# Clustered attention and a gated convolution FFN on one core: q loaded with three tokens in a row to a partition, and exponentials that write their columns back into sequence

## The chip, the core and the metric

The kernel runs on one core of a Trainium2 chip. The metric is the device time in microseconds (us) of one execution. The core has TensorE (PE, with its weight loads shown apart as PEld), VectorE (DVE), ScalarE (ACT), GpSimd (POOL), SyncE (SP), which here only issues DMAs, and 16 DMA engines.

## The reference

Four batches, eight heads, 768 tokens, head size 64. Each token of q and of k belongs to the nearest of 16 centroids of its head; a query sees the keys of its own cluster only. The output of the attention goes through a feed-forward layer with a convolution over three tokens and a gate.

```python
q_assign = np.argmax(np.einsum('bhsd,hcd->bhsc', q_n, c_n), axis=-1)
k_assign = np.argmax(np.einsum('bhsd,hcd->bhsc', k_n, c_n), axis=-1)
mask = q_assign[:, :, :, None] == k_assign[:, :, None, :]
scores = np.where(mask, scale * np.matmul(q, k.transpose(0, 1, 3, 2)), -1e9)
attn = softmax(scores)                       # over the keys
x = np.matmul(attn, v)                       # heads put side by side: 512 columns
h = np.maximum(x @ w_in, 0.0)                # 1024 columns
conv_out = conv_w[0] * h[s-1] + conv_w[1] * h[s] + conv_w[2] * h[s+1]
out = (h * sigmoid(conv_out)) @ w_out
```

The order of the keys does not matter as long as k and v have the same one. The order of the queries is that of the output, and of the convolution.

## The kernel before

**Pairs and slots.** The work goes by pairs of heads: pair g is two heads of one batch, 16 pairs in all. A slot t is half of the queries (384, HS) of one pair, 32 slots in all; `slot` gives a slot's batch, half a, and pair. Batch 0 is slots 0 to 7 and batch 1 slots 8 to 15. Each slot has six steps i: head i // 3, and a third of the keys (two blocks of 128).

**Loads and transposes.** q and k come from the device's memory with tokens on partitions (qk_in) and are needed with the 64 columns of a head on partitions (qkT, then ext in f16). Two ways lead there. Pairs 7 to 15 (`in_blocks`, those for which the plan has an LZ step) are loaded as blocks of 32 by 32 and turned by VectorE (L298). Pairs 0 to 6 are loaded by `load_q` and `load_k` (L255 and L263), transposed by TensorE (`transposes`, L309), 128 tokens of two blocks at a time, copied from PSUM to qkT by ScalarE or VectorE (L315, L317), and cast into ext (L330). For these seven pairs k is loaded with six tokens in a row to a partition, so that k's columns in ext are in a permuted order, and v alike (L279). q is loaded token by token: partition p gets the tokens p, 128 + p, 256 + p and so on, and the columns of q are in sequence.

**Clusters.** The argmax over the centroids (L347 to L389) runs on the columns as they stand, and three more rows of ext (partitions 64 to 66) carry the cluster of each token, so that a matmul of ext with ext gives the masked score; the partitions behind are zero.

**Scores, exponentials, values.** `scores` (L437) multiplies two blocks of keys by the 384 queries of the slot into one of two PSUM tiles sc, in turn. `exps` (L450) takes exp of such a tile, 128 x 768 values, into two rows of attn in f16 (L454). `values` (L461) loads 128 columns of attn as weights and multiplies them by v, so that the 128 queries of a column block become the partitions of the result (L466); `normalize` divides by the sum, and a transpose brings x to xT, whose columns are tokens in sequence. The feed-forward layer (L520 on) reads xT.

**What sets the order.** PLAN is one list of steps written out; each engine runs the instructions of its steps in that order, and each queue of DMAs is in that order too. Nothing reorders them. In PLAN, LQ and L are loads of q (and k), T transposes, Qa and Qd the copies to qkT, CD the casts into ext, S scores, E exponentials, V values, LV and CV the load and cast of v. The first step of the plan is the load of q of pair 0, head 0.

Of the kernel before, what the change touches and what calls it, by code (L numbers as in the profile page):

```python
# [10 lines left out]
AF = mybir.ActivationFunctionType  # L11
# [144 lines left out]
def kernel(  # L156
# [11 lines left out]
    nc = tc.nc  # L168
    B, H, S, D = q.shape
    P = 128  # L170
# [6 lines left out]
    HS = S // 2  # L177
# [2 lines left out]
    SPB = 2 * NPR  # L180
    NU = 2 * NPR
    BR = 3
    SHARP = 24.0


# [11 lines left out]
    sc = [psum.tile([P, 2, 512], F32, name=f"sc{i}") for i in range(2)]  # L197
# [22 lines left out]
    NE = 6  # L220
    ext_b = [const.tile([P, 2, 2, S], F16, name=f"ext{i}") for i in range(NE)]
# [14 lines left out]
    def batch_pair(g):  # L236
        return g // NPR, 2 * (g % NPR)

    def heads(h):
        return slice(0, 2) if h is None else slice(h, h + 1)  # L240

    def qk_in(g):
        if g not in qk_t:
            qk_t[g] = rot.tile([P, 2, 2, J, D], F32, name="qk_in", tag="qk_in", bufs=4)
        return qk_t[g]
# [4 lines left out]
    in_blocks = [f"LZ.{g}.0" in PLAN for g in range(B * NPR)]  # L250
# [4 lines left out]
    def load_q(g, h=None, queue=nc.sync):  # L255
        b, h0 = batch_pair(g)
        hs = heads(h)
        queue.dma_start(
            qk_in(g)[:, 0, hs].rearrange("p h j d -> p (h j) d"),
            q[b, h0 + hs.start : h0 + hs.stop].rearrange("h (j p) d -> p (h j) d", p=P),  # L260
        )

    def load_k(g, h=None, queue=nc.sync):  # L263
# [55 lines left out]
    def copy(name, to, src):  # L319
        if name == "a":  # L320
            nc.scalar.activation(to, src, AF.Copy)
        else:
            (nc.vector if name == "d" else nc.gpsimd).tensor_copy(out=to, in_=src)  # L323
# [32 lines left out]
    def argmax(g, h, i):  # L356
# [24 lines left out]
        else:  # L381
# [3 lines left out]
            if i == 5:  # L385
                nc.vector.tensor_scalar(out=mid, in0=best, scalar1=-8.5, scalar2=SHARP, op0=ALU.add, op1=ALU.mult)
            else:
# [20 lines left out]
    def bias_rows(g, h, queue=nc.sync):  # L408
        n = 6 * J * (1 if h is not None else 2)
        queue.dma_start(  # L410
            ext_b[g % NE][D : D + BR, heads(h)].rearrange("r h a s -> r (h a s)"), spk_t.pop((g, h))[0:n, :]
        )


    def turn_rows(g, h, a, at):
        turn_at[g, h, a] = at
        for j in range(J):
            nc.tensor.transpose(
                bank16[at][D : D + BR, P * j : P * (j + 1)], pack_v[h][:, a : 2 * BR : 2, j], id16[:]
            )  # L420

    def rows_copy(name, g, h, a):
        copy(name, ext_b[g % NE][D : D + BR, h, a, :], bank16[turn_at[g, h, a]][D : D + BR, 0:S])

    attn, x16, x_at, av_at = {}, {}, {}, {}
# [4 lines left out]
    def slot(t):  # L432
        b, i = divmod(t, SPB)
        a, pr = SLOTS0[i] if b == 0 else divmod(i, NPR)
        return b, a, pr, b * NPR + pr

    def scores(t, i):  # L437
        b, a, pr, g = slot(t)
        h, kt = i // 3, 2 * (i % 3)
        s = sc[(6 * t + i) % 2]  # L440
        for n in range(2):
            nc.tensor.matmul(  # L442
                s[:, n, 0:HS],
                lhsT=ext_b[g % NE][:, h, 1, P * (kt + n) : P * (kt + n + 1)],
                rhs=ext_b[g % NE][:, h, 0, HS * a : HS * (a + 1)],
                start=True,
                stop=True,
            )

    def exps(t, i):  # L450
        if i % 3 == 0:
            attn[t, i // 3] = rot.tile([P, J, HS], F16, name="attn", tag="attn", bufs=4)
        kt = 2 * (i % 3)
        nc.scalar.activation(  # L454
            attn[t, i // 3][:, kt : kt + 2, :], sc[(6 * t + i) % 2][:, :, 0:HS], AF.Exp, scale=0.125
        )

    def avp(at):
        return bank[at][:, 0 : J * VW].rearrange("p (u w) -> p u w", u=J)
# [193 lines left out]
    def setup(name, i, j):  # L653
# [54 lines left out]
        elif name == "pk":  # L708
            n = pack_n[i]
            nc.gpsimd.memset(pack_b[i][:, 6 * n * J : P], 0.0)  # L710
            for h in range(n):
                nc.gpsimd.memset(pack_v[i][:, 2 * h + 1 : 2 * h + 4 * n + 1 : 4 * n - 1], -SHARP / 2)
        elif name == "v":
# [38 lines left out]
    def step(token):  # L752
# [5 lines left out]
        if name[0] == "_":  # L758
            setup(name[1:], at if at is not None else x[0] if x else 0, last)
        elif name == "L":  # L760
            load_q(x[0])
            load_k(x[0])
        elif name == "LQ":
            load_q(x[0], last)
        elif name == "LK":
            load_k(x[0], last)
# [30 lines left out]
        elif name == "BA":  # L797
            bias_rows(x[0], last, nc.scalar)
        elif name == "S":
            scores(*x)  # L800
        elif name == "E":
            exps(*x)
        elif name == "V":
            values(*x, at)
# [67 lines left out]
```

## Time and profile before

| what | value |
|---|---|
| median of 3 runs | 240.79 us (240.72 to 243.44) |
| profiled execution | 240.68 us |
| its span, first to last instruction | 238.9 us |
| granted TensorE clock over the span | 0.998 |
| exponentials (L454) | 192 of 128 x 768, 817 ns each by the mean |
| loads of q of pairs 0 to 6 | 4 of 192 KB and 5 of 384 KB |
| packets of all DMAs | 102,958, of which 94,603 under 512 B |

In the profile's rows L and a number is a line of the kernel. "out<-in" are the names of tiles without their buffer numbers. In a list of groups, "x192 | 146.4, 817 | 4.0 <-PE sc L442 2.7" reads: 192 instructions, 146.4 us busy, 817 ns each, 4.0 us in which the engine sat idle just before one of them, 2.7 of it ended by PE's writing of sc in line 442. The chain that ended last is followed back from the last instruction, at each step to what released it. "issue" is idle time for which the profile shows no releaser.

### The profile page before, as it was taken

What the parts mean: (1) busy time and instruction counts of PE and PEld (TensorE: products, weight loads), DVE (VectorE), ACT (ScalarE), POOL (GpSimd) and SP (SyncE); (2) the same over time, 40 slices, a digit from 0 to 9 for tenths busy, and PEclk for the clock granted to TensorE, in tenths of its full rate; (3) what the DMA queues carried; (4) which work ended last, traced back from release to release, by engine and by line L of the source; (5) the groups of instructions that cost most, each with busy time, mean ns of one, the idle gap of its engine ahead of it and who ended that gap; (6) DMA issues with size and microseconds to landing.
All of it is one profiled execution on the core that took longest, in us unless ns stands there. A gap on an engine that the chain in (4) does not pass through costs nothing.

```text
span 238.9 us, 6438 instructions
## 1 busy us (share of the span) xinstructions
PE 227.7 (95%) x2442; PEld 143.5 (60%) x2442; DVE 215.4 (90%) x497; ACT 215.4 (90%) x337; POOL 84.6 (35%) x149
## 2 busy tenths in 40 slices
PE   7988998999999999999999999999999999999984
PEld 4665665575556566655666666655776666555531
DVE  6999999989999999999899999999899999983850
ACT  5998997999999999999999999999999999994542
POOL 8559664790168335411935031304540001000000
PEclk9999999999999999999999999999999999999999
DMA  7988599944956975878669507890542110323104
GB/s 198 294 243 257 157 233 245 323 80 83 242 92 136 183 128 94 173 126 183 163 150 169 114 3 188 153 134 1 168 89 63 33 47 16 105 64 112 68 0 177
DMA packets 102958, 32.77 MB, mean 137 GB/s; under 512 B 94603, under 2 KB 98187, under 8 KB 102926
## 3 DMA queue, kind: packets, MB, share of 16 engines
q1 hardware_dynamic: 102599, 32.11, 57.3%
q8 instruction: 19, 0.31, 0.6%
q10 hardware_dynamic: 327, 0.24, 0.4%
q14 instruction: 13, 0.11, 0.1%
HBM read 23.11 MB, written 6.29 MB: 123 GB/s over the span
## 4 chain that ended last, share of the span: by engine, by line
PE 64%; DVE 15%; ACT 12%; POOL 5%; issue 2%; DVEq 0%; POOLq 0%
PE sc L442 17%; PE flex L524 15%; PE flex L604 14%; PE flex L466 10%; ACT attn L454 8%; PE flex L347 3%; POOL ext L323 3%; PE sc L566 3%; ACT th L584 2%; DVE best L380 1%; DVE ext L323 1%; DVE cnv L560 1%; DVE x L480 1%; PE sc L604 1%; DVE val L377 1%
## 5 line engine op out<-in xcount | busy, mean ns | idle before, releaser
L454 ACT ACTIVATE attn<-sc 128x768 f16<-128x768 f32 x192 | 146.4, 817 | 4.0 <-PE sc L442 2.7
L442 PE MATMUL sc<-ext 128*128 128x384 f16 x384 | 89.3, 325 | 3.8 <-ACT attn L454 2.1
L466 PEld LDWEIGHTS <-attn 128*128 128x128 f16 x1152 | 50.5, 97 | 15.2 <-ACT attn L454 0.4
L560 DVE SCALAR_TENSOR_TENSOR cnv<-hpad,cwcol,cnv 128x382 f16<-128x382 f16 (+1 forms) x100 | 58.4, 609 | 0.4
L323 POOL CAST ext<-qkT 64x768 f16<-64x768 f32 x48 | 41.7, 875 | 40.6 <-DVE qkT L298 20.0
L466 PE MATMUL flex<-v,attn 128*128 128x65 f16 x1152 | 54.5, 193 | 0.3 <-ACT attn L454 0.3
L524 PE MATMUL flex<-xT,w_in 128*128 128x384 f16 x256 | 49.1, 326 | 0.1
L442 PEld LDWEIGHTS <-ext 128*128 128x128 f16 x384 | 32.5, 97 | 26.9 <-issue 9.2
L604 PE MATMUL flex<-w_out,hg 128*128 128x512 f16 x176 | 47.1, 379 | 0.0
L592 DVE SCALAR_TENSOR_TENSOR hg<-th,hpad 128x764 f16<-128x764 f32 (+2 forms) x33 | 30.7, 934 | 3.1 <-ACT th L584 3.0
L524 PEld LDWEIGHTS <-w_in 128*128 128x128 f16 x256 | 23.9, 98 | 15.6 <-issue 0.6
L604 PEld LDWEIGHTS <-hg 128*128 128x128 f16 x192 | 17.9, 98 | 16.8 <-DVE hg L592 1.1
L537 ACT ACTIVATE hpad<-flex 128x384 f16<-128x384 f32 x45 | 21.8, 501 | 2.4 <-PE flex L524 1.6
L323 POOL CAST v<-v_in 128x768 f16<-128x768 f32 x15 | 14.6, 977 | 24.7 <-DMA v_in<-in_v_dram 24.6
L584 ACT ACTIVATE th<-cnv 128x764 f32<-128x764 f16 (+1 forms) x25 | 21.2, 848 | 0.7 <-DVE cnv L560 0.7
L323 POOL COPY hpad<-hf 128x6 f16<-128x6 f16 x12 | 4.9, 418 | 42.0 <-DVE hg L592 41.8
L480 DVE TENSOR_TENSOR x<-flex,rec 128x384 f16<-128x384 f32 x32 | 17.8, 558 | 1.1
L298 DVE STREAM_TRANSPOSE qkT<-qk_in 128x768 f32<-128x768 f32 x18 | 17.3, 966 | 0.0
L558 DVE TENSOR_SCALAR cnv<-hpad,cwcol 128x382 f16<-128x382 f16 (+1 forms) x50 | 16.3, 349 | 0.6 <-ACT hpad L537 0.5
L323 POOL COPY hf<-hpad 128x6 f16<-128x6 f16 x11 | 3.6, 329 | 30.7 <-ACT hpad L537 18.6
L347 PE MATMUL flex<-qkT,cT 128*32 128x192 f32 x256 | 14.1, 333 | 0.0
L309 PE MATMUL flex<-id,qk_in 128*128 128x128 f32 x84 | 12.5, 287 | 1.2 <-ACT qkT L315 0.6
(82 smaller groups left out, 217.1 us busy)
## 6 DMA issues: line engine op xcount, KB each, us to landing
v_in<-in_v_dram SPq DMA_DIRECT2D x16, 384.0 KB
out_dram<-o_sb SPq DMA_DIRECT2D x24, 256.0 KB
qk_in<-in_q_dram SPq DMA_DIRECT2D x36, 96.0 KB
qk_in<-in_k_dram SPq DMA_DIRECT2D x36, 96.0 KB
qk_in<-in_q_dram SPq DMA_DIRECT2D x5, 384.0 KB
qk_in<-in_k_dram SPq DMA_DIRECT2D x5, 384.0 KB
w_sb<-in_moe_w_out_dram SPq DMA_DIRECT2D x2, 768.0 KB
w_sb<-in_moe_w_in_dram SPq DMA_DIRECT2D x3, 512.0 KB
```

The lines of the kernel that those rows point to most:

```text
L323: (nc.vector if name == "d" else nc.gpsimd).tensor_copy(out=to, in_=src)
L347: nc.tensor.matmul(bank[at][32 * j : 32 * (j + 1), 192 * i : 192 * (i + 1)], lhsT=cT32[:, which, :], rhs=tokens[:, j], start=True, stop=Tr ...
L442: nc.tensor.matmul(s[:, n, 0:HS], lhsT=ext_b[g % NE][:, h, 1, P * (kt + n) : P * (kt + n + 1)], rhs=ext_b[g % NE][:, h, 0, HS * a : HS * ( ...
L454: nc.scalar.activation(attn[t, i // 3][:, kt : kt + 2, :], sc[(6 * t + i) % 2][:, :, 0:HS], AF.Exp, scale=0.125)
L466: nc.tensor.matmul(avp(at)[:, u, 0 : D + 1], lhsT=attn[t, h][:, kt, P * jq : P * (jq + 1)], rhs=v16_b[g % NE][:, h, kt, 0 : D + 1], start= ...
L480: nc.vector.tensor_tensor(out=x16[t].rearrange("p jq (h d) -> p h jq d", h=2), in0=av[:, :, 0:D].rearrange("p (h jq) d -> p h jq d", h=2), ...
L524: nc.tensor.matmul(bank[at][:, 0:HS], lhsT=w_in16[:, r, 2 * u + f, :], rhs=xT[:, b % 2, r, HS * a : HS * (a + 1)], start=(r == 0), stop=(r ...
L537: nc.scalar.activation(to, src, AF.Relu)
L560: nc.vector.scalar_tensor_tensor(out=cnv, in0=src, scalar=w, in1=cnv, op0=ALU.mult, op1=ALU.add)
L584: nc.scalar.activation(th_t[n][:, fs, 0:N], pre[:, fs, 0:N], AF.Tanh, scale=0.5)
L592: nc.vector.scalar_tensor_tensor(out=hg_b[b][:, 2 * u + fs.start : 2 * u + fs.stop, LO[a] : LO[a] + N], in0=th_t[n][:, fs, 0:N], scalar=1. ...
L604: nc.tensor.matmul(bank[at][:, 0:Dm], lhsT=hg_b[b][:, fb, P * tq : P * (tq + 1)], rhs=w_out16[:, fb, :], start=(fb == 0), stop=(fb == NFB ...
```

## The change

Three edits, of which the second leaves the operand as it was (KR is 128).

```diff
+    KR = P
...
         queue.dma_start(
-            qk_in(g)[:, 0, hs].rearrange("p h j d -> p (h j) d"),
-            q[b, h0 + hs.start : h0 + hs.stop].rearrange("h (j p) d -> p (h j) d", p=P),
+            qk_in(g)[:, 0, hs].rearrange("p h (a j) d -> p (h a) (j d)", a=2),
+            q[b, h0 + hs.start : h0 + hs.stop].rearrange("h (a p j) d -> p (h a) (j d)", a=2, j=3),
         )
...
-                lhsT=ext_b[g % NE][:, h, 1, P * (kt + n) : P * (kt + n + 1)],
-                rhs=ext_b[g % NE][:, h, 0, HS * a : HS * (a + 1)],
+                lhsT=ext_b[g % NE][0:KR, h, 1, P * (kt + n) : P * (kt + n + 1)],
+                rhs=ext_b[g % NE][0:KR, h, 0, HS * a : HS * (a + 1)],
...
-        nc.scalar.activation(
-            attn[t, i // 3][:, kt : kt + 2, :], sc[(6 * t + i) % 2][:, :, 0:HS], AF.Exp, scale=0.125
-        )
+        to, src = attn[t, i // 3][:, kt : kt + 2, :], sc[(6 * t + i) % 2][:, :, 0:HS]
+        if not in_blocks[slot(t)[3]]:
+
+            to, src = to.rearrange("p n (x j) -> p n j x", j=3), src.rearrange("p n (j x) -> p n j x", j=3)
+        nc.scalar.activation(to, src, AF.Exp, scale=0.125)
```

In each half a of the queries, partition p now holds the tokens 384 a + 3 p, + 1 and + 2, which lie behind one another in the device's memory: a packet of the load is 3 x 64 x 4 = 768 B in place of 256 B. After the transposes, column 128 j + x of the half is token 3 x + j. The scores come out in that order, and the exponential puts column (j, x) into column 3 x + j of attn. It reads PSUM in sequence and writes f16 values 6 B apart, in six runs of 128 (two blocks of keys by three j). Behind it everything is in sequence, as before. The exponentials of pairs 7 to 15 stay as they were.

No instruction is added, removed or moved on any engine. ScalarE's first exponentials, with what stands between them, before (tile names with their buffer numbers; the number at the end is the shape written):

```order
L454 ACTIVATE attn<-sc_66 128x768
L315 ACTIVATE qkT<-flex_68 128x512
L315 ACTIVATE qkT<-flex_69 128x512
L315 ACTIVATE qkT<-flex_71 128x512
L454 ACTIVATE attn<-sc_67 128x768
L454 ACTIVATE attn<-sc_66 128x768
```

and in the changed kernel:

```order
L459 ACTIVATE attn<-sc_66 128x2x3x128
L316 ACTIVATE qkT<-flex_68 128x512
L316 ACTIVATE qkT<-flex_69 128x512
L316 ACTIVATE qkT<-flex_71 128x512
L459 ACTIVATE attn<-sc_67 128x2x3x128
L459 ACTIVATE attn<-sc_66 128x2x3x128
```

Only the shape of the write is another one; the order is the same.

## The prediction

> **What bounds the kernel now.** I read the page first: the span, the engines' busy shares and the chain that ended last.
>
> ```profile
> span 238.9 us, 6438 instructions
> PE 227.7 (95%) x2442; PEld 143.5 (60%) x2442; DVE 215.4 (90%) x497; ACT 215.4 (90%) x337; POOL 84.6 (35%) x149
> ...
> PE 64%; DVE 15%; ACT 12%; POOL 5%; issue 2%; DVEq 0%; POOLq 0%
> ...
> L454 ACT ACTIVATE attn<-sc 128x768 f16<-128x768 f32 x192 | 146.4, 817 | 4.0 <-PE sc L442 2.7
> ```
>
> Three engines are busy for 90% or more of the span, so none has much slack. The exponentials (L454) are 146.4 of ScalarE's 215.4 us; all but 4.0 us of the time before them was filled. The next view is the busy time by stretches. The columns are the stretch, its length, then busy us and instruction count of PE, PEld, DVE, ACT and POOL, the granted clock, the DMA share and GB/s.
>
> ```profile
> core 0: us, PE busy (x) PEld busy (x) DVE busy (x) ACT busy (x) POOL busy (x), PEclk, DMA share, GB/s
> 0.00:12.00 12.00, 10.18 (x86) 6.50 (x86) 9.69 (x29) 9.10 (x18) 8.06 (x35) 1.00 0.94 246
> 12.00:25.00 13.00, 11.22 (x125) 7.87 (x118) 12.51 (x38) 11.82 (x20) 9.71 (x17) 1.00 0.78 233
> 25.00:40.00 15.00, 14.15 (x190) 10.22 (x187) 14.55 (x38) 14.65 (x22) 9.58 (x14) 1.00 0.91 226
> 40.00:55.00 15.00, 14.00 (x198) 9.20 (x196) 13.49 (x29) 13.80 (x21) 10.59 (x18) 1.00 0.70 184
> 55.00:70.00 15.00, 14.12 (x149) 8.48 (x147) 14.53 (x38) 14.23 (x24) 2.62 (x4) 1.00 0.73 156
> 70.00:85.00 15.00, 14.67 (x158) 9.05 (x157) 14.79 (x33) 15.00 (x24) 9.42 (x12) 1.00 0.80 153
> 85.00:100.00 15.00, 14.91 (x218) 10.36 (x215) 14.69 (x37) 14.33 (x23) 6.01 (x9) 1.00 0.68 123
> ```
>
> From 12 to 100 us, where the changed exponentials lie, ScalarE is busy 11.82 + 14.65 + 13.80 + 14.23 + 15.00 + 14.33 = 83.8 of 88 us. It has 4.2 us of idle time there. Whatever an exponential costs more than now is swallowed only up to those 4.2 us.
>
> The DMA engines are also busy, 0.94 of the first 12 us, so I asked whether anybody waits for them. The two lists below are what PE's transposes of q and k (L309) sat idle for, and the one wait of a compute engine for a load in the list of waits.
>
> ```profile
> its engine sat idle before it (us, times) until:
>   ACT qkT L315: 1.6, 2
>   DVE xT L499: 0.9, 2
>   ACT ext L321: 0.6, 2
>   issue: 0.5, 2
>   DVE sim L364: 0.3, 1
>   DVE cwcol L734: 0.3, 1
> ```
>
> ```profile
> POOL v L323 <- DMA v_in<-in_v_dram: 24.6, 6, 10.3
> ```
>
> The transposes are the only readers of q as it is loaded, and no row of theirs ends on a DMA; at most the 0.5 us of "issue", which names no releaser, could hide one. The only load that is waited for is v's, on GpSimd, which is busy 35% of the span. The chain of waits at the start says what sets it instead:
>
> ```profile
> 2.88 0.70 DVE ext L716
> 3.61 0.24 DVE sq_c L672
> 3.87 0.23 DVE nrm_c L673
> 4.13 0.20 ACT nrm_c L675
> 4.35 1.28 ACT L700
> 5.64 0.20 ACT scratch L700
> 5.84 0.39 ACT qkT L315
> ```
>
> VectorE's clearing of ext, the norm of the centroids and ScalarE's second table load come first, and the copies of q's and k's transposes (L315) start only behind that load, at 5.8 us. By then the first transposes, which ran from 4 us on, are waiting to be copied.
>
> **The change part by part.** *The loads of q.* Nothing moves in any engine's order. The seven pairs have 7 x 2 heads x 768 tokens = 10,752 packets of 256 B; three tokens in a row make them 3,584 packets of 768 B. The DMA view of the first 14 us prices a packet:
>
> ```profile
> DMA packets 8699, 3.52 MB, mean 251 GB/s; under 512 B 7666, under 2 KB 8695, under 8 KB 8698
> ...
> q1 hardware_dynamic: 8410, 3.27, 89.3%
> ```
>
> That is 0.893 x 16 x 14 us / 8410 = 23.8 ns per packet of one engine. If a packet of 768 B took no longer than that mean, 7,168 fewer would save 7,168 x 23.8 ns / 16 = 10.7 us of the DMA engines' time; if time goes by bytes, nothing. Somewhere between lies DMA time that no engine waits for, covered by the ACT and DVE work quoted above. On the path I bound the gain by 0 and by the 0.5 us of "issue" ahead of the transposes, and take the upper end, 0.5 us, since the DMA engines really are full there. If the cover were gone the start would still wait for the table load. The loads of k and v behind q on SP's queue go out earlier too; GpSimd's wait for v shrinks, but GpSimd waits for other work afterwards, so I cost that at nothing.
>
> The Trainium skill (DMA: Bandwidth & Descriptors, Specifications) puts the smallest transfer at line rate at 512 B, so that q would leave the slow side and come out on the fast one. No run here shows it yet; by it the saving would be nearer 10.7 than 0 us of DMA time, and the sum the same, since nobody waits for q.
>
> *The exponentials.* The pairs that TensorE transposes are g = 0 to 6: 8 slots of batch 0 and 6 of batch 1, so 14 x 6 = 84 of the 192. This view counts the exponentials by stretch:
>
> ```profile
> 0.00:25.00 25.00, 5.49 (x7) 1.00 0.85 240
> 25.00:50.00 25.00, 21.55 (x30) 1.00 0.89 234
> 50.00:75.00 25.00, 19.22 (x26) 1.00 0.62 125
> 75.00:100.00 25.00, 17.87 (x23) 1.00 0.78 146
> ```
>
> So 86 start by 100 us, six of them (slot 11) of a pair in blocks; nearly all of the 84 lie there. Each still reads 768 f32 of PSUM one behind the other, but it writes six runs of 128, each element 6 B behind the last, where it wrote rows of 2 B steps. No ScalarE row of this trace writes with a step. The nearest, of ScalarE by form:
>
> ```profile
> L454 ACT ACTIVATE attn<-sc 128x768 f16<-128x768 f32 x192 | 146.4, 817 | 4.0 <-PE sc L442 2.7
> L537 ACT ACTIVATE hpad<-flex 128x384 f16<-128x384 f32 x45 | 21.8, 501 | 2.4 <-PE flex L524 1.6 <-DVE hg L592 0.2
> L584 ACT ACTIVATE th<-cnv 128x764 f32<-128x764 f16 x13 | 10.9, 836 | 0.0
> ...
> L321 ACT ACTIVATE ext<-qkT 64x768 f16<-64x768 f32 x7 | 5.9, 842 | 0.1
> ...
> L584 ACT ACTIVATE th<-sc 128x764 f32<-128x764 f32 x3 | 2.4, 807 | 0.7 <-PE sc L566 0.7
> ```
>
> (817 - 501) / 384 = 0.823 ns for each element. Two things follow. First, runs of 128 are cheap: the copy into ext (L321, 842 ns) writes six runs of 128 and the tanh (L584 from cnv, 836 ns) writes unbroken rows of 764, both from SBUF; 4 elements are 3.3 of the 6 ns, so the breaks cost about 3 ns. Second, the write side has room: the tanh from PSUM writes 4 B for each element in 807 ns, the exponential 2 B in 817 ns. Twice the bytes, and twice the addresses passed over, cost nothing.
>
> A step of 6 B passes over 1.5 times the addresses of that f32 write. Lower end: no price beyond the breaks, 84 x 3 ns = 0.25 us. A gain is excluded, because the element rate is the same for every form here. Upper end, if the write side were just full at 4 B for each element: half as long again per element, 0.5 x 0.823 x 768 = 316 ns each, 84 x 316 = 26.5 us. I take the lower end, since the f32 write is the nearest row in addresses passed over, and it is free.
>
> No row here shows a step of 6 B, and the Trainium skill (SBUF — State Buffer, section Door 1: The DMA port swizzle) gives a rule for it: lines of 16 B, and full bandwidth as long as each line takes at least two hits in a row. A 6 B step gives two or three hits per line, so so by the page, which counts 8 bf16 elements as the reach of a free step, the price is nothing and the sum is unchanged.
>
> *The rest.* 0:KR is 0:128, the same operand as before. PE's weight loads read attn exactly where they did; x comes out in sequence. These cost nothing. The semaphores of a few DMAs change; each waits on SP behind a load that was issued well ahead, and I cost it at nothing.
>
> The sum goes against the profiled execution, 240.68 us, which is a span of 238.9 and 1.8 us around it and 0.1 under the median of the runs: 240.68 - 0.5 + 0.25 = 240.4 us.
>
> **The rivals.** *A: the step has a price on ScalarE.* Place: the 84 exponentials between 13 and about 101 us. For it: no row has such a write, and ScalarE has little slack. The chain of waits shows the exponentials in it back to back:
>
> ```profile
> 61.68 4.10 ACT attn L454 x6
> 65.83 0.82 ACT attn L454
> 66.69 0.48 PE sc L442 x2
> ```
>
> PE can't run ahead, since only two score buffers exist: the scores behind an exponential (L442) wait for its end. Against it: the f32 rows. It decides from 4.8 us, 2% of 240.8: 57 ns for each if all of it shows (7% of an exponential), (4.8 + 4.2) / 84 = 107 ns if the idle time swallows its 4.2 us. At 316 ns the time is 240.4 + 26.5 = 266.9 us, or 262.7 with the idle time filled: 265. At half that price, 158 ns, it is 240.4 + 13.3 = 253.7 us at most.
>
> *B: the start is bound by the loads after all.* For it: the DMA share of 0.94. Against it: the transposes' idle rows. Its ceiling is PE's idle time to 25 us, (12 - 10.18) + (13 - 11.22) = 3.6 us, which gives 240.68 - 3.6 = 237.1 us, still within 2%. Faster by over 2% needs more than that: the wait for v (24.6 us on GpSimd) would have to matter as well.
>
> *C: nothing at all happens*, neither the 0.5 nor the 0.25 us: 240.7 us. It can't be told from the forecast and counts with it.
>
> **How the numbers follow.** Forecast with C: 0.55. B, within 2%: 0.06. Together 0.61 for within 2%, which is about what a measurement of this kernel can tell from no change. Rival A: 0.34, because the one operation that changes on a full engine has no row; 0.19 of that for a price up to 158 ns and 0.15 for more. Faster by over 2%: 0.05. The range starts at 238.0, leaving out the faster case, and ends at 254.0, where A at half its price ends; what lies outside is 0.05 + 0.15 = 0.20. The forecast's own range is 238.0 to 242.5. The predicted time is 240.4 us.
>
> **What would show it.** Right: L454's forms with four dimensions at 810 to 825 ns beside the unchanged form, fewer packets under 512 B by about 10,750, ScalarE's busy time within 1 us of 215.4, and the chain at the start still through the table load at 4.35 us. Wrong: the new form 60 ns or more above the old one, with PE's scores waiting on "ACT attn" by tens of us between 13 and 101 us (A); or transposes and first copies that start earlier by more than 0.5 us (B).

## The result and the profile after

The changed kernel takes 283.56 us (median of 4 runs, 283.32 to 283.58) where the one before takes 242.12 (240.72 to 243.50, 4 runs): 1.171 times as long, 95% interval 1.162 to 1.180. The forecast was 240.4 us, within 2%; the time lies beyond the range's end of 254 and beyond both sizes given for rival A.

The page of the kernel after, the rows that answer to those of before:

```profile
span 281.5 us, 6438 instructions
...
PE 236.4 (84%) x2442; PEld 146.4 (52%) x2442; DVE 217.1 (77%) x497; ACT 262.0 (93%) x337; POOL 80.9 (29%) x149
...
ACT 45%; PE 40%; DVE 8%; issue 5%; ACTq 0%; DVEq 0%
...
L459 ACT ACTIVATE attn<-sc 128x768 f16<-128x768 f32 x192 | 195.8, 1112 | 1.8 <-PE sc L443 1.0
L443 PE MATMUL sc<-ext 128*128 128x384 f16 x384 | 91.8, 329 | 35.2 <-ACT attn L459 33.4
```

ScalarE's busy time rose by 262.0 - 215.4 = 46.6 us, and its part of the chain from 12% to 45%. The exponentials' mean of 1112 ns mixes two kinds: with the 108 unchanged ones at 817, the 84 changed ones took (1112 x 192 - 817 x 108) / 84 = 1491 ns, 674 more than before. TensorE's scores now sit idle for them: 33.4 us.

The stretches of the kernel after show how full ScalarE is while the changed exponentials run (columns as in the prediction):

```profile
25.00:40.00 15.00, 9.50 (x124) 6.46 (x124) 10.19 (x27) 15.00 (x16) 6.83 (x11) 1.00 0.62 163
40.00:55.00 15.00, 10.09 (x115) 6.41 (x114) 8.20 (x23) 15.00 (x12) 3.75 (x7) 1.00 0.66 198
...
85.00:100.00 15.00, 10.86 (x106) 6.30 (x106) 7.40 (x16) 15.00 (x13) 3.82 (x6) 0.77 0.22 37
```

ScalarE is busy for all of each 15 us; before, PE, DVE and ACT shared the bound here. From 85 to 100 us the granted TensorE clock is 0.77, where it was 1.00 before; PE is busy for 10.86 of these 15 us and ScalarE for all of them, so this is not where the time is lost. The waits of the kernel after, and below it the same wait before:

```profile
PE sc L443 <- ACT attn L459: 33.4, 63, 1.4
```

```profile
PE sc L442 <- ACT attn L454: 2.1, 6, 0.8
```

The sums close as follows. 84 x 674 ns are 56.6 us. ScalarE's busy time grew by 46.6 only, because neighbours overlap, and the new ones by more than the old. Sixteen of the new ones in a row take 20.75 us, 1.30 us from one to the next (first line); ten of the old ones took 7.72 us, 0.77 us from one to the next (second line, the kernel before). Where they stand in a row a new one costs 0.53 us more, and 84 x 0.53 = 44.5 us is most of the 46.6. Of these 46.6 the span shows 281.5 - 238.9 = 42.6; the other 4.0 went into ScalarE's idle time, which fell from 23.5 to 19.5 us.

```profile
39.79 20.75 ACT L459 ACTIVATE attn<-sc 128x768 f16<-128x768 f32 x16
```

```profile
32.16 7.72 ACT L454 ACTIVATE attn<-sc 128x768 f16<-128x768 f32 x10
```

### The profile page after: what moved, and what is told of

It is laid out like the page before. It is cut to its first block, busy times and chain, and to the rows that moved or that the text cites. A ratio compares the mean times of both kernels' runs of the same rounds, so it can differ in the third digit from the quotient of the medians.

```text
span 281.5 us, 6438 instructions
## 1 busy us (share of the span) xinstructions
PE 236.4 (84%) x2442; PEld 146.4 (52%) x2442; DVE 217.1 (77%) x497; ACT 262.0 (93%) x337; POOL 80.9 (29%) x149
## 2 busy tenths in 40 slices
DMA packets 95790, 32.77 MB, mean 116 GB/s; under 512 B 83851, under 2 KB 91019, under 8 KB 95758
## 4 chain that ended last, share of the span: by engine, by line
ACT 45%; PE 40%; DVE 8%; issue 5%; ACTq 0%; DVEq 0%
ACT attn L459 34%; PE flex L607 10%; PE sc L443 10%; PE flex L527 8%; PE flex L469 6%; ACT th L587 2%; ACT hpad L540 2%; PE sc L569 2%; DVE cnv L563 1%; ACT qkT L316 1%; DVE hg L595 1%; ACT ext L322 1%; PE flex L348 1%; PE sc L607 1%; ACT o_sb L620 1%
## 5 line engine op out<-in xcount | busy, mean ns | idle before, releaser
L459 ACT ACTIVATE attn<-sc 128x768 f16<-128x768 f32 x192 | 195.8, 1112 | 1.8 <-PE sc L443 1.0
L443 PE MATMUL sc<-ext 128*128 128x384 f16 x384 | 91.8, 329 | 35.2 <-ACT attn L459 33.4
L443 PEld LDWEIGHTS <-ext 128*128 128x128 f16 x384 | 34.5, 98 | 63.2 <-issue 47.7
L324 POOL CAST ext<-qkT 64x768 f16<-64x768 f32 x48 | 40.6, 853 | 83.6 <-PE sc L443 32.2
L563 DVE SCALAR_TENSOR_TENSOR cnv<-hpad,cwcol,cnv 128x382 f16<-128x382 f16 (+1 forms) x100 | 59.7, 623 | 0.4
L469 PEld LDWEIGHTS <-attn 128*128 128x128 f16 x1152 | 51.4, 98 | 16.0 <-issue 1.2
L469 PE MATMUL flex<-v,attn 128*128 128x65 f16 x1152 | 55.4, 195 | 0.7 <-ACT attn L459 0.7
L482 DVE RECIPROCAL rec<-flex 128x6 f32<-128x6 f32 x32 | 5.9, 185 | 17.9 <-PE flex L469 17.9
L324 POOL CAST v<-v_in 128x768 f16<-128x768 f32 x15 | 12.7, 852 | 20.5 <-DMA v_in<-in_v_dram 20.3
L365 DVE STREAM_TRANSPOSE sim<-flex 128x384 f32<-128x384 f32 (+1 forms) x18 | 9.7, 536 | 8.9 <-PE flex L348 8.7
```

The costliest lines, as they stand in the source:

```text
L443: nc.tensor.matmul(s[:, n, 0:HS], lhsT=ext_b[g % NE][0:KR, h, 1, P * (kt + n) : P * (kt + n + 1)], rhs=ext_b[g % NE][0:KR, h, 0, HS * a : ...
L459: nc.scalar.activation(to, src, AF.Exp, scale=0.125)
L469: nc.tensor.matmul(avp(at)[:, u, 0 : D + 1], lhsT=attn[t, h][:, kt, P * jq : P * (jq + 1)], rhs=v16_b[g % NE][:, h, kt, 0 : D + 1], start= ...
L563: nc.vector.scalar_tensor_tensor(out=cnv, in0=src, scalar=w, in1=cnv, op0=ALU.mult, op1=ALU.add)
```

## The experiments

### Which of the two edits

The load alone:

```diff
-        if not in_blocks[slot(t)[3]]:
-            to, src = to.rearrange("p n (x j) -> p n j x", j=3), src.rearrange("p n (j x) -> p n j x", j=3)
```

> The load of q in threes alone; the exponentials write rows as before, so the queries of the seven pairs come out in the permuted order. Theory (the write with a step costs ScalarE about twice the time, and the load is hidden): within 1 us of the kernel before, 239.5 to 241 us against 240.7, and the new form of the exponential is gone (810 ns). Rival (the new load, or what comes earlier because of it, is what costs): a good part of the 42 us stays, 260 us or more. By the prediction's term for the load: 0.5 us faster.

Measured 240.84 us (12 runs) against 241.16: ratio 0.9999 (0.9974 to 1.0023). The load shows no cost and no gain; the interval reaches 0.3% either way. The step alone, which is the same two lines put into the kernel before, without the new load:

> The write with a step of 6 B alone; q is loaded token by token, so the order of the queries of the seven pairs is wrong in the output. Theory: 282 to 285 us, all of the loss, with 84 exponentials at about 1490 ns. Rival (load): 241 us.

One run: 283.58 us, span 281.8. All of the loss is in the write. Its row of ScalarE from 30 to 60 us, where the exponentials are changed ones (first line), is that of the changed kernel (second line) within 7 ns:

```profile
L458 ACT ACTIVATE attn<-sc 128x768 f16<-128x768 f32 x23 | 30.2, 1501 | 0.0
```

```profile
L459 ACT ACTIVATE attn<-sc 128x768 f16<-128x768 f32 x23 | 30.2, 1494 | 0.0
```

### The pattern or the step

Six runs, no step:

```diff
+            to, src = to.rearrange("p n (j x) -> p j n x", j=3), src.rearrange("p n (j x) -> p j n x", j=3)
```

> The kernel before, with each of the 84 exponentials read and written in six runs of 128 in another order of runs, each run without a step. Theory (the step of 6 B is what costs, not the pattern): 240.5 to 241.5 us, the form at 810 to 830 ns. Rival (a pattern of four dimensions, or the breaks, cost): near 283 us, the form at about 1490 ns, or in between if the breaks are a part.

A step of two elements:

```diff
+            to, src = to.rearrange("p n (x j) -> p n j x", j=2), src.rearrange("p n (j x) -> p n j x", j=2)
```

> The kernel before, with the 84 exponentials written with a step of two elements (4 B) in place of three; the queries of the seven pairs are put in a wrong order by it. Theory a (two f16 values side by side share one turn of the write, and any step breaks the pairs): as 6 B, about 1490 ns and 283 us. Theory b (the price goes by the addresses passed over, and 4 B for each element is free as it is for f32): 810 to 830 ns and 241 us. Between them: a price that grows with the step, about 1150 ns and 262 us.

The exponentials of the two, the one with six runs first:

```profile
L457 ACT ACTIVATE attn<-sc 128x768 f16<-128x768 f32 x192 | 146.3, 816 | 3.4 <-PE sc L442 1.9
```

```profile
L457 ACT ACTIVATE attn<-sc 128x768 f16<-128x768 f32 x192 | 162.9, 939 | 1.9 <-PE sc L442 1.0
```

Breaking the write into six runs of 128 is free (816 ns; 242.69 us in one run, among the runs of before, 239.94 to 243.65). The step of 4 B is not: (939 x 192 - 817 x 108) / 84 = 1096 ns for each changed exponential, 251.46 us in one run. Neither "any step costs the same" (283 us) nor "4 B is free as it is for f32" (241 us) holds. The case between them, a price that grows with the step, was near in the exponential (1150 ns) and not in the time (262 us).

### A price list

So I measured the disputed cost by itself, with copies behind the kernel's last step.

```diff
+    for _ in range(3):
+        nc.scalar.activation(w16[:, 0:N], ps[:, 0:N], AF.Copy)
+        nc.scalar.activation(w16[:, 0 : 2 * N : 2], ps[:, 0:N], AF.Copy)
+        nc.scalar.activation(w16[:, 0 : 3 * N : 3], ps[:, 0:N], AF.Copy)
...
```

> The kernel before, with rows of copies of 384 elements put behind its last step, three times over: on ScalarE f16 writes from PSUM with steps of 2, 4, 6, 8 and 16 B, f16 pairs 12 B apart, f32 writes with steps of 4, 8, 12 and 16 B, reads of PSUM with steps of 8 B and of 512 B, reads of SBUF with steps of 2, 6 and 16 B; on VectorE a few of the same. The contiguous f16 copy from PSUM should take about 500 ns. Theory a (a 2-byte write that does not stand beside its neighbour takes a second turn): all f16 steps about 820 ns, the pairs about 500, all f32 steps about 500, all reads about 500. Theory b (price by addresses passed over): grows from 500 with the step, alike for f16 and f32 at the same step, and the pairs about as 6 B.

The list, ScalarE. The lines are, from L849: f16 written with steps of 2, 4, 6, 8 and 16 B; L854 f16 pairs side by side, a pair every 12 B; L855 to L858 f32 with steps of 4, 8, 12 and 16 B; L859 and L860 PSUM read with steps of 8 and 512 B; L861 to L863 SBUF read with steps of 2, 6 and 16 B (f16).

```profile
L853 ACT ACTIVATE ext<-sc 128x384 f16<-128x384 f32 x3 | 5.6, 1865 | 0.1
L852 ACT ACTIVATE ext<-sc 128x384 f16<-128x384 f32 x3 | 3.1, 1018 | 0.1
L863 ACT ACTIVATE ext<-ext 128x384 f16<-128x384 f16 x3 | 2.6, 875 | 0.1
L858 ACT ACTIVATE ext<-sc 128x384 f32<-128x384 f32 x3 | 2.5, 842 | 0.1
...
L857 ACT ACTIVATE ext<-sc 128x384 f32<-128x384 f32 x3 | 2.0, 675 | 0.1
L851 ACT ACTIVATE ext<-sc 128x384 f16<-128x384 f32 x2 | 1.6, 807 | 0.1
L862 ACT ACTIVATE ext<-ext 128x384 f16<-128x384 f16 x3 | 1.6, 523 | 0.1
L861 ACT ACTIVATE ext<-ext 128x384 f16<-128x384 f16 x3 | 1.6, 522 | 0.1
L856 ACT ACTIVATE ext<-sc 128x384 f32<-128x384 f32 x3 | 1.5, 507 | 0.1
L854 ACT ACTIVATE ext<-sc 128x384 f16<-128x384 f32 x3 | 1.5, 498 | 0.1
L855 ACT ACTIVATE ext<-sc 128x384 f32<-128x384 f32 x3 | 1.5, 491 | 0.1
...
L860 ACT ACTIVATE ext<-sc 128x384 f16<-128x384 f32 x3 | 1.5, 490 | 0.1
L850 ACT ACTIVATE ext<-sc 128x384 f16<-128x384 f32 x2 | 1.2, 596 | 0.1
L849 ACT ACTIVATE ext<-sc 128x384 f16<-128x384 f32 x2 | 1.0, 490 | 0.1
```

Single f16 values cost 490, 596, 807, 1018 and 1865 ns as the step grows, while f32 values at 8 B cost 507 and at 12 B 675. Both theories fail: the price grows with the step (against a), but not alike for the two types, and pairs 12 B apart are free although they pass over the same addresses as singles 6 B apart (against b). The reading side is almost free: PSUM with 512 B jumps 490 ns, SBUF with 6 B steps 523; only 16 B steps in SBUF cost (875).

A second list asked what the pairs meant and whether the price goes on growing.

```diff
+        nc.scalar.activation(w16[:, 0:3072:32], ps[:, 0:96], AF.Copy)
+        nc.scalar.activation(pairs(1, 8, 2), two, AF.Copy)
...
```

> The kernel before with a second list of ScalarE copies from PSUM to f16 behind its last step, three times over. The first list gave about 0.55 ns for each element and each 2 B of step where that is more than the 0.83 ns of an element, and no price for pairs 12 B apart. Theory a (the step between neighbours in the innermost run sets the price, and a run of two that stand side by side hides the jump behind it): 96 elements 16 B apart take about 0.17 + 96 x 4.4 ns = 590 ns, 32 B apart 1020, 64 B apart 1860; pairs side by side 16 and 32 B from the next pair about 500 ns; pairs with 4, 6 and 12 B between the two, one pair every 14 or 16 B, 600 to 1300 ns. Theory b (pairs were free because both fall into one word of 4 B, and everything else goes by the addresses passed over): pairs every 16 and 32 B cost about 0.17 + 3.07/3.63 = 1.0 us and 1.9 us or their half, and two side by side that straddle a word (from an odd element) cost about as two. Theory c (the price stops growing at a line of some size): 32 and 64 B apart cost as 16 B, 590 ns. Three in turn, 256 B apart, of 768: under a far above 1.5 us, under c about 3.5 us.

Here L852 to L854 are 96 elements 16, 32 and 64 B apart; L855 and L856 pairs side by side every 16 and 32 B; L857 two values 4 B apart every 14 B, L859 two values 12 B apart every 16 B; L860 pairs from an odd element, so that they straddle words of 4 B, every 8 B; L863 768 values 6 B apart; L864 768 values, three in turn, 256 B apart.

```profile
L864 ACT ACTIVATE ext<-sc 128x768 f16<-128x768 f32 x3 | 10.8, 3595 | 0.1
...
L863 ACT ACTIVATE ext<-sc 128x768 f16<-128x768 f32 x3 | 4.3, 1443 | 0.1
L859 ACT ACTIVATE ext<-sc 128x384 f16<-128x384 f32 x3 | 3.1, 1018 | 0.1
L857 ACT ACTIVATE ext<-sc 128x384 f16<-128x384 f32 x3 | 2.7, 914 | 0.1
...
L860 ACT ACTIVATE ext<-sc 128x384 f16<-128x384 f32 x3 | 1.8, 597 | 0.1
L856 ACT ACTIVATE ext<-sc 128x384 f16<-128x384 f32 x3 | 1.5, 514 | 0.1
L852 ACT ACTIVATE ext<-sc 128x96 f16<-128x96 f32 x2 | 1.2, 594 | 0.1
L854 ACT ACTIVATE ext<-sc 128x96 f16<-128x96 f32 x2 | 1.2, 586 | 0.1
```

The price stops growing at 16 B: 594 ns there and 586 at 64 B, as theory c said and against a. Pairs in whole words stay nearly free up to the 32 B tried (514 ns, against 490 in sequence), pairs that straddle words do not (597 ns), against b. From the two lists I formed one rule for copies from PSUM. The figures come out as if ScalarE's write worked in lines of 16 B and words of 4 B. Each time the stream enters another line it pays 4.41 ns if it leaves words half written, and 1.74 ns if it writes whole words; each element takes 0.83 ns; the larger of the two sums counts, and 170 ns come on top. The two prices are slopes of the first list: (1865 - 1018) / (384 - 192 lines) = 4.41 and, f32, (842 - 675) / (384 - 288) = 1.74. The table shows how well the rule fits the lists from which it was formed; it is no test of it.

| copy | lines entered | by the rule, ns | measured, ns |
|---|---|---|---|
| 384 f16, step 4 B | 96 | 96 x 4.41 + 170 = 593 | 596 |
| 384 f16, step 6 B | 144 | 805 | 807 |
| 384 f32, step 8 B | 192 | 192 x 1.74 + 170 = 504 | 507 |
| two values every 14 B | 168 | 911 | 914 |
| two values, 12 B apart, every 16 B | 192 | 1017 | 1018 |
| straddling pairs every 8 B | 96 | 593 | 597 |
| 768 f16, step 6 B | 288 | 1440 | 1443 |
| 768 f16, 256 B apart | 768 | 3557 | 3595 |

### The rule tested in the kernel

The rule says that the same addresses, passed in the same three turns, are free if whole words are written:

```diff
+            to = to.rearrange("p n (x j i) -> p j n x i", j=3, i=2)
+            src = src.rearrange("p n (j x i) -> p j n x i", j=3, i=2)
```

> The kernel before, with the 84 exponentials written as pairs side by side, each pair 12 B behind the last, in three passes; it passes over the same addresses as the step of 6 B and opens as many lines of 16 B, 288 for 768 elements. The queries of the seven pairs are put in a wrong order by it. Theory (the two lists fit 4.41 ns for each line of 16 B that is opened with half-written words, 1.75 ns where whole words of 4 B are written, against 0.83 ns for each element; the larger sum counts): 288 x 1.75 = 504 ns is less than 768 x 0.83 = 640 ns, so 810 to 830 ns for the form and 240.5 to 243 us. Rival (lines opened are what costs, however full the words): 288 x 4.41 = 1270 ns, about 1490 ns and 283 us. An exponential in the running kernel might also pay for what other engines do, which would give something between.

The exponentials, and ten changed ones in a row:

```profile
L458 ACT ACTIVATE attn<-sc 128x768 f16<-128x768 f32 x192 | 148.6, 832 | 3.3 <-PE sc L442 1.9
```

```profile
34.83 7.70 ACT L458 ACTIVATE attn<-sc 128x768 f16<-128x768 f32 x10
```

(832 x 192 - 817 x 108) / 84 = 851 ns, 34 more than before and 640 less than with a step of 6 B; 243.55 us in one run. Both lie above what was expected, by 21 ns and by 0.55 us. The rival is ruled out: the addresses and the lines are those of the step of 6 B, and the whole words take the price away. Ten in a row take 7.70 us, as before (7.72), so the 34 ns do not slow ScalarE where it is full. In the running kernel the rule gives too little, by 10 to 79 ns: it gives 807 ns for rows and for these pairs, 1017 for the step of 4 B and 1440 for that of 6 B, where 817, 851, 1096 and 1491 were measured. What the rest is paid for is open.

This run had its first exponential at 16.0 us and not at 13.5, as the run with six runs had (242.69 us) and the profiled one of the load alone (243.30 us). It is to be compared with these two, and is 0.25 to 0.86 us longer. The last section shows this start.

### Putting the order right elsewhere

If only the write is dear, the exponential can read with jumps and write in sequence:

```diff
-            to, src = to.rearrange("p n (x j) -> p n j x", j=3), src.rearrange("p n (j x) -> p n j x", j=3)
+            to, src = to.rearrange("p n (x j) -> p n x j", j=3), src.rearrange("p n (j x) -> p n x j", j=3)
```

> The changed kernel, but the exponential writes attn in sequence and reads PSUM with the jumps instead: 512 B from one element to the next, three in turn. Theory (only the write of 2-byte elements with a step costs): 817 ns for each exponential, and the time of the load alone, 239.5 to 241 us. Rival (any step on ScalarE costs, or PSUM's side costs as much): about 1490 ns and 283 us.

```profile
L458 ACT ACTIVATE attn<-sc 128x768 f16<-128x768 f32 x192 | 146.4, 817 | 3.5 <-PE sc L443 2.1
```

817 ns, and 240.88 us (12 runs) against 241.25: ratio 1.0002 (0.9970 to 1.0034). The whole loss is gone by changing the order of two loops in the access pattern. Or TensorE can stream q's columns in sequence:

```diff
+        qs = ext_b[g % NE][0:KR, h, 0, HS * a : HS * (a + 1)]
+        if not in_blocks[g]:
+            qs = qs.rearrange("p (j x) -> p x j", j=3)
```

> The changed kernel, but TensorE puts the order right: the scores of the seven pairs stream q's columns out of ext with jumps of 256 B, and the exponentials read and write rows. Theory (the step costs ScalarE alone): 239.5 to 241 us. Rival (TensorE's stream pays for jumps too): the 168 matmuls of 325 ns take up to twice as long, 27 us at 0.16 us each, of which most shows, 255 to 268 us.

```profile
L446 PE MATMUL sc<-ext 128*128 128x384 f16 x384 | 124.8, 420 | 1.2 <-DVE ext L324 0.8 <-ACT attn L459 0.2
...
ACT attn L459 <- PE sc L446: 21.8, 51, 1.2
```

269.18 us (6 runs), ratio 1.121 (1.116 to 1.127), a little beyond the 268 of the rival. The 168 changed matmuls took (420 x 384 - 325 x 216) / 168 = 542 ns in place of 325, and now ScalarE waits for them, 21.8 us. The rival had the cause right: TensorE's stream pays for jumps of 256 B in SBUF.

## Why the prediction was wrong, point by point

- **The step that failed** is "I take the lower end, since the f32 write is the nearest row in addresses passed over, and it is free". The f32 rows write whole words; the change writes half words. What fits the copies from PSUM is how many lines of 16 B are entered and whether words are left half written, not the addresses passed over. 288 lines at 4.41 ns are 1.27 us against 0.64 us of elements. In the kernel the changed exponential took 674 ns more, where the sum had 3, and the term of 84 x 3 ns = 0.25 us turned out as 46.6 us of ScalarE's time, 42.6 of them in the span.
- **The upper end failed too.** 316 ns was worked out from a limit "just full at 4 B for each element", for whole words and half words alike. No row of before held a write of single f16 values, so no bound could be drawn from f32. A doubling of the element's time, 632 ns, was not ruled out by any row and would have carried the range past 283 us. It would have done so by luck: 674 ns were measured, and the time stays inside such a range only because neighbours overlap, so that each shows 0.53 us in a row.
- **The rule of the Trainium skill** (SBUF — State Buffer, section Door 1: The DMA port swizzle), two hits in a line of 16 B are enough, was cited for the write. The runs disagree there: f16 steps of 4 B (four hits a line) already cost 596 ns against 490. For ScalarE's reads of SBUF they agree with the two hits: 523 ns at 6 B, as in sequence (522), and 875 ns at 16 B, one hit a line. The reach of 8 elements that the prediction took from there would include that step of 16 B, and it was not free. I had weighed the rule as if it covered both sides.
- **Rival A** named the right place, the right engine and the right wait ("PE's scores waiting on ACT attn by tens of us"), at a price of half its true size and a chance of 0.34.
- **The idle time** was sized well, and in the right place: 4.2 us from 12 to 100 us were said to be swallowed. In the kernel after, ScalarE is idle for 0.3 us from 12 to 145 us, and over the span its idle time fell by 4.0.
- **The breaks** (3 ns for each) were right: six runs are free.
- **The loads**: nobody waits for q, as said, and the packets under 512 B fell from 94,603 to 83,851, by the 10,752 forecast. The 0.5 us of "issue" ahead of the transposes is still there in the kernel after and in the one that reads with jumps; in both the first exponential starts at 13.5 us, as before. So no trace shows the 0.5 us forecast, and a term of that size is too small for the times to show. In the kernel that reads with jumps, the DMA share of the first 12 us fell from 0.94 to 0.85, and the DMA engines' time on q1 from 57.3% of 238.9 us to 55.8% of 238.7, 3.7 us; the load of v goes out at 9.2 us, not 12.9. That is inside the 0 to 10.7 given, and nearer to 0, not to 10.7 as the sentence on 512 B had it.

## What to carry to other kernels

A price for an access pattern must come from a row with the same element size and the same side: what f32 shows says nothing on half words, and what a read shows nothing on a write. When a permutation has to sit in an instruction of a full engine, list both ends of that instruction: here the jump was free on the PSUM read and cost 17% of the kernel on the f16 write. And where no row of the trace shows the operation, a range drawn from its neighbours is no bound, and neither is a doubling: the changed exponential took 1491 ns for 817, and a copy with a step of 16 B took 1865 for 490.

## What the runs showed of the hardware that was not expected

In the lists, ScalarE's writes of single f16 values fit 4.41 ns for each line of 16 B entered, and those of whole words 1.74 ns. VectorE pays as well: a copy of 384 from PSUM to f16 takes 558 ns in sequence (L866) and 796 ns with a step of 6 B (L867), f16 to f16 in SBUF 259 and 489 (L870, L871).

```profile
L867 DVE CAST ext<-sc 128x384 f16<-128x384 f32 x3 | 2.4, 796 | 0.1
...
L866 DVE CAST ext<-sc 128x384 f16<-128x384 f32 x3 | 1.7, 558 | 40.6 <-ACT ext L864 40.5
```

The start has two courses. In the kernel with six runs and no step, TensorE's three transposes at 6.28 us took 0.90 us, and 0.55 us in the kernel before; the rest of its work up to 14 us was slower in the same way. The first exponential then came at 16.0 us, and the span was 2 us longer:

```profile
5.17 0.90 PE L309 MATMUL flex<-id,qk_in 128*128 128x128 f32 x3 [0.36 <-DMA qk_in<-in_k_dram]
...
6.28 0.90 PE L309 MATMUL flex<-id,qk_in 128*128 128x128 f32 x3
```

```profile
6.28 0.55 PE L309 MATMUL flex<-id,qk_in 128*128 128x128 f32 x3 [0.61 <-ACT qkT L315]
```

There a load of k had come late (0.36 us of wait), and so it had in the kernel with pairs (0.35 us). In the profile of the load alone the first exponential came at 16.0 us too, with no such wait, and the granted clock is 1.00 in both courses, so the cause stays open. It may be behind the kernel before's spread of 240.7 to 243.5 us; no run tested that.
